# The feed-forward block by pairs of units, with the transposes ahead of a pair, a second ACT read of their bank, and later input loads

## The chip, the cores and the metric

The kernel runs on one core of a Trainium2 chip. It drives five engines: PE (matrix products, with a separate weight-load row PEld), DVE (vector), ACT (activations), POOL (GpSimd, which here issues weight loads and does a few additions) and SP (which issues most transfers). The metric is the time of one launch in device microseconds; lower is better. Three timed runs of the kernel before are at hand and one profiled execution.

## The reference

The input x is 2048 rows of 640 numbers, fp32. Everything after the layer norm works on the normalised rows:

```python
xn = _layernorm(x, axis=-1)
s = _A_ref(xn, A_wqkv, A_wo)          # attention, then @ wo
g = _silu(_B_ref(xn, B_w1, B_w2))     # silu(silu(xn @ w1) @ w2), 640 -> 1536 -> 640
return x + s * g
# in _A_ref: 32 heads of 20; each row attends to 8 rows, itself and every second row before it
qkv = x @ wqkv
logits = einsum("bhsd,bhswd->bhsw", q, kg) * 20 ** -0.5     # masked before row 0
o = einsum("bhsw,bhswd->bhsd", softmax(logits), vg)
return o @ wo
```

## The kernel before, in words

The 2048 rows are cut into four groups of 512 (two halves, even and odd rows). A group is worked as four tiles of 128 rows. Every product is computed to nearly fp32 precision from two halves, high and low: `TH` and `TL` hold the transposed activations (two copies of each, one for the present group and one for the next group or for the attention output), `WR` is a ring of seven slots, each with the high and low half of one weight unit, and a product is three matmuls: high by high, low by high, high by low.

A group goes through three phases on PE:

- `qkv_phase`: four quarters (8 heads each) of five chunks; a chunk is four tiles of three matmuls of 480 columns (L638 to L640). ACT reads the banks into `kv` and `q` (`evac_qkv`, L444 and L447), `halo` (L458 on) shifts rows between partitions by transfers, and `scores` and `values` (L481 to L521) compute the attention on DVE, with an exponential on ACT (L496) in between. In the quarters of a group the attention output of the group before is transposed chunk by chunk (`o_chunk`, placed by `O_AT`).
- `wo_phase`, from the second group on: the output projection of the group before, 20 tiles of six matmuls (L672 and L674). DVE multiplies the result by the gate `G` (L704), POOL adds x (L711), SP stores (L713).
- `ffn_phase`: 12 units f. An "up" (L791 to L793) is 15 matmuls of 512 columns into one of two `rot` banks; ACT reads the bank twice with silu, to `sh` (high half, L797) and `sf` (full, L798), and DVE subtracts to get `sl` (L799). A "down" multiplies `sh` (16 matmuls, "big") and then `sl` (8 matmuls, "small") into six `acc` banks, which hold the whole group's 512 by 640 result. Before the change the order on PE is up 0, up 1, down 0, up 2, down 1, and so on to up 11, down 10, down 11, so that up f is two units ahead of down f. At the end ACT takes the gate's silu out of the six banks (L828).

During `ffn_phase` the next group's five transposes of x are made, one before each of up 7 to up 11 (`split_t`: four PE transposes into a `rot` bank at L433, the high half by ACT at L437, the low half by DVE at L438 from the same bank). The last group has no next x; in the same way it transposes the attention output of its own group before up 8 to up 11 and before down 11 (`OL_AT`). The rows of the next group are loaded into `XIN` (`load_x`, L404) and normalised on DVE and ACT (`ln_stats`, `ln_rstd`, `ln_apply`).

No order is written out by hand for the engines other than PE. A planner, `Weave`, holds all operations with their reads, writes, a duration from a formula and a priority. PE's order is the program's; for DVE, ACT, POOL and SP it goes through time and takes at each step the operation that could start first, and among those the one of lowest priority number. The order that it finds is then fixed: on the chip each engine works through its list and waits where an operand is not ready. Priority 0 have the evacuations and `sl`, 1 the layer norm, 50 the splits of weights, 100 and up the attention.

Weight units are read from DRAM as fp32 (`raw_load`, L346, into `PR`, `RAW` and `G` early on, later `RAW` alone), split once by ACT (L372) and DVE or POOL (L378), stored as halves (L384), and read back as halves by POOL's queue when the unit comes again (L364). The tiles `XR` hold rows of x for the final addition (L710).

Of the kernel before, what the change touches and what calls it, by code (L numbers as in the profile page):

```python
# [8 lines left out]
F32 = mybir.dt.float32  # L9
# [5 lines left out]
P = 128  # L15
# [7 lines left out]
T = 4  # L23
# [10 lines left out]
HALVES = 1  # L34
BY_ACT = (1,)
QAT = 48
X_AT = 3, 6, 8
TILE_AT = 1, 1.5, 5, 6
LOW_AT = 3
# [134 lines left out]
def local_attention_silu_ffn(ctx: ExitStack, tc: tile.TileContext, x, wqkv, wo, w1, w2, out):  # L174
# [82 lines left out]
    def dma(fn, reads, writes, nbytes, prio, dur=0.45):  # L257
        add("SP", dur, fn, reads, writes, prio, nbytes=nbytes)
# [15 lines left out]

    units = []
    for g in range(NG):
        units += [("q", q, c) for q in range(NQ) for c in range(DC)]
        if g:  # L280
            units += [("wo", c) for c in range(DC)]
        for f in range(FC + 1):
            if f < FC:
                units.append(("w1", f))
            if f:
                units.append(("w2", f - 1))
    units += [("wo", c) for c in range(DC)]
    again = {u: sum(v == u for v in units) for u in units}
    halves = {}
# [25 lines left out]
    def raw_load(k):  # L315
# [7 lines left out]
        if k < DC:  # L323
            r, kr = PR.rearrange("p t w m -> p (t w m)")[:, k * n:(k + 1) * n], [PRK[k]]
        elif k < early:
            s = (k - DC) % 6
            r, kr = (RAW[s], [("raw", s)]) if s < 2 else (G[:, s - 2, :], [("g", s - 2, 0), ("g", s - 2, CA)])
            r = r[:, :n]
        else:
            s = k % 2  # L330
            r, kr = RAW[s][:, :n], [("raw", s)]
        raws[i] = r, kr
        if u[0] == "q":
            _, q, c = u
# [66 lines left out]


    def load_x(g, t, n=1, prio=None):
        dma(lambda: nc.sync.dma_start(XIN[:, t:t + n], rows(xg, g)[:, t:t + n]), [],  # L404
            [("xin", u) for u in range(t, t + n)], n * P * D * 4, clock[0] if prio is None else prio)

    def ln_stats(t, after=()):
# [19 lines left out]
    def split_t(src, skeys, c, i):  # L427

        ps, kp = rot()

        def turn():
            for t in range(T):
                nc.tensor.transpose(ps[:, tsl(t)], src[:, t, c * P:(c + 1) * P], ident)  # L433
# [3 lines left out]
        act(TOK, lambda: nc.scalar.activation(hi, ps, AF.Copy), [kp], kh, 0)  # L437
        dve(TOK, lambda: nc.vector.tensor_tensor(out=lo, in0=ps, in1=hi.bitcast(F32), op=OP.subtract),  # L438
            [kp] + kh, kl, 0)


    def evac_qkv(g, q, t, ps, kp):
# [181 lines left out]
    def qkv_phase(g, i, io):  # L624
        for q in range(NQ):
# [34 lines left out]
    OL_AT = {8: 0, 9: 1, 10: 2, 11: 3, 12: 4}  # L660
    XT_AT = 7

    def tm_banks():
        a = [bank() for t in range(T)]
# [99 lines left out]
        leave(t, B)  # L764

    def ffn_phase(g, i, ix, io):
        nxt = g + 1 if g + 1 < NG else None
        ps = prev = None
        for f in range(FC + 1):
            if nxt is not None and f == 0:  # L770
                load_x(nxt, 0, 2)
                load_x(nxt, 2, 2)
                for t in range(T):
                    ln_stats(t)
                ln_rstd(0, T)
                for t in range(T):
                    ln_apply(t)
            if nxt is not None and XT_AT <= f < XT_AT + DC:
                split_t(XIN, [("xin", t) for t in range(T)], f - XT_AT, ix)
            if nxt is None and f in OL_AT:  # L780
                o_chunk(g, OL_AT[f], io)
            cur = None
            if f < FC:
                wh, wl, kh, kl = w_next("w1", f)
                h, kp = rot()
                s = f % 2

                def first(wh=wh, wl=wl, h=h):
                    for c in range(DC):
                        cs = tsl(c)  # L790
                        nc.tensor.matmul(h, wh[:, cs], TH[i][:, c, :], start=c == 0, stop=False)  # L791
                        nc.tensor.matmul(h, wh[:, cs], TL[i][:, c, :], start=False, stop=False)  # L792
                        nc.tensor.matmul(h, wl[:, cs], TH[i][:, c, :], start=False, stop=c == DC - 1)  # L793
                pe(15 * mm(TOK), first, t_keys(i, range(DC)) + [kh, kl], [kp])
                w_done()
                sf, sh, sl = SF[s], SH[s], SL[s]
                act(TOK, lambda sh=sh, h=h: nc.scalar.activation(sh, h, AF.Silu), [kp], [("sh", s)], 0, "silu")  # L797
                act(TOK, lambda sf=sf, h=h: nc.scalar.activation(sf, h, AF.Silu), [kp], [("sf", s)], 0, "silu")  # L798
                dve(TOK, lambda sf=sf, sh=sh, sl=sl: nc.vector.tensor_tensor(  # L799
                    out=sl, in0=sf, in1=sh.bitcast(F32), op=OP.subtract), [("sf", s), ("sh", s)], [("sl", s)], 0, lock=True)  # L800
                cur = sh, sl, ("sh", s), ("sl", s)
            if f:
                sh, sl, ksh, ksl = prev
                if ps is None:
                    ps = tm_banks()
                a, b = ps
                wh, wl, kh, kl = w_next("w2", f - 1)
                for t in range(T):
                    def big(t=t, f=f, wh=wh, wl=wl, sh=sh):
                        tm_mm(ps, t, sh[:, tsl(t)], wh, f == 1, False)  # L810
                        tm_mm(ps, t, sh[:, tsl(t)], wl, False, False)

                    def small(t=t, f=f, wh=wh, sl=sl):
                        tm_mm(ps, t, sl[:, tsl(t)], wh, False, f == FC)
                    ko = [a[t][1], b[t // 2][1]]
                    pe(2 * TM, big, [ksh, kh, kl], ko)
                    if f == FC:
                        pe(TM, small, [ksl, kh], ko)
                    else:
                        late.append((TM, small, [ksl, kh], ko))  # L820
                for args in late:
                    pe(*args)
                late.clear()
                w_done()
            prev = cur
        for p, kp, ts, cs in tm_views(ps):
            n = (ts.stop - ts.start) * (cs.stop - cs.start)
            act(n, lambda p=p, ts=ts, cs=cs: nc.scalar.activation(G[:, ts, cs], p, AF.Silu), [kp], gkeys(ts, cs), 0, "silu")  # L828

    late = []  # L830
# [41 lines left out]
```

## Time and profile before

| what | value |
|---|---|
| timed runs | 641.08, 641.50, 641.52 us, median 641.5 |
| the profiled execution, its own time | 641.25 us |
| its span, first to last instruction | 639.5 us |
| granted PE clock | 1.000 |
| PE busy | 632.2 us |
| DVE busy | 540.1 us |
| ACT busy | 204.1 us |
| POOL busy | 122.3 us |
| transfers | 162.44 MB, mean 254 GB/s |

The span is what the profile's records cover; the execution's own time is 1.75 us longer. A row of a group view gives line, engine, operation, the tile written and the tile read, shapes, the count, the busy time, the mean duration of one, and the idle time of the engine just before with what ended it. In a timeline a row is a start, a duration and the same names. Successive instructions of one engine overlap a little in these records, on PE by design: the distance between starts, not the duration, is what a matmul costs there.

### The profile page before, as it was taken

To read this page: it belongs to the slowest core of one execution; us is meant where nothing else is said; L and a number is where in the kernel's file an instruction comes from. 1 tells how busy PE (TensorE), PEld (TensorE's weight loads), DVE (VectorE), ACT (ScalarE), POOL (GpSimd) and SP (SyncE) were. 2 spreads that over 40 slices of the span, in tenths; PEclk is the share of its full clock that TensorE was granted. 3 is DMA by queue.
4 is the path that set the end of the run, shared out by engine and by line. 5 is a ranking of instruction groups with operands and counts; after the bars stand their busy time and mean duration, and the time that the engine had idled before them with its cause. 6 is when DMAs were issued, how large, how long until landed. Compare 5 with 4: busy or idle time off the path is not lost.

```text
span 639.5 us, 9016 instructions
## 1 busy us (share of the span) xinstructions
PE 632.2 (99%) x3495; PEld 572.2 (89%) x3495; DVE 540.1 (84%) x539; ACT 204.1 (32%) x399; POOL 122.3 (19%) x168
## 2 busy tenths in 40 slices
PE   7999999999999999999999999999999999999997
PEld 6888889999889989999888999999988899899997
DVE  7699999999999899999859999999106999999714
ACT  5436453443524023232422112223313222233230
POOL 4500000001101241111222124311222213311100
PEclk9999999999999999999999999999999999999999
DMA  9999998787999998657699976965679996876522
GB/s 283 336 307 337 338 372 327 298 280 237 280 285 327 318 310 258 197 163 218 179 270 272 297 214 207 359 201 162 171 207 265 276 315 202 284 272 189 183 83 82
DMA packets 74154, 162.44 MB, mean 254 GB/s; under 512 B 5648, under 2 KB 47088, under 8 KB 74112
## 3 DMA queue, kind: packets, MB, share of 16 engines
q0 software_dynamic: 26672, 82.58, 44.7%
q1 hardware_dynamic: 46896, 78.88, 39.6%
q8 instruction: 27, 0.44, 0.3%
q10 hardware_dynamic: 544, 0.41, 0.2%
q14 instruction: 15, 0.12, 0.1%
HBM read 109.55 MB, written 34.16 MB: 225 GB/s over the span
## 4 chain that ended last, share of the span: by engine, by line
PE 97%; DVE 1%; DMA 1%; ACT 0%; issue 0%
PE acc L672 22%; PE acc L674 15%; PE acc L638 10%; PE acc L639 10%; PE acc L640 10%; PE rot L793 9%; PE rot L791 9%; PE rot L792 9%; PE rot L433 2%; PE acc L583 2%; DMA xin<-in_A_x_dram 1%; DVE st L548 1%; DVE xin L553 0%; PE rot L761 0%; PE rot L562 0%; DVE tl L570 0%
## 5 line engine op out<-in xcount | busy, mean ns | idle before, releaser
L638 PE MATMUL acc<-w,th 128*128 128x480 f32 x300 | 114.7, 382 | 0.0
L672 PE MATMUL acc<-w,sh 128*128 128x384 f32 x384 | 113.6, 335 | 0.0
L639 PE MATMUL acc<-w,tl 128*128 128x480 f32 x300 | 113.5, 378 | 0.0
L640 PE MATMUL acc<-w,th 128*128 128x480 f32 x300 | 113.4, 378 | 0.0
L674 PE MATMUL acc<-w,sh 128*128 128x256 f32 x384 | 107.1, 279 | 0.0
L481 DVE TENSOR_TENSOR pr<-q,kv 128x2560 f32<-128x2560 f32 x32 | 90.3, 2821 | 11.7 <-DMA kv<-kv 11.3
L791 PE MATMUL rot<-th,w 128*128 128x512 f32 x240 | 95.4, 398 | 0.0
L793 PE MATMUL rot<-th,w 128*128 128x512 f32 x240 | 94.0, 391 | 0.0
L792 PE MATMUL rot<-tl,w 128*128 128x512 f32 x240 | 93.8, 391 | 0.0
L513 DVE TENSOR_TENSOR pr<-e,kv 128x2560 f32<-128x2560 f32 x32 | 90.3, 2823 | 0.8
L484 DVE TENSOR_REDUCE l<-pr 128x128 f32<-128x2560 f32 x32 | 90.0, 2813 | 0.2
L364 POOL DMA_DIRECT2D w<-half_q x52 | 37.3, 717 | 233.4 <-PE rot L793 122.5
L518 DVE TENSOR_TENSOR pr<-pr 128x1280 f32<-128x1280 f32 x64 | 78.3, 1224 | 1.1
L797 ACT ACTIVATE sh<-rot 128x512 fp32r<-128x512 f32 x48 | 28.8, 599 | 151.5 <-PE rot L793 151.4
L674 PEld LDWEIGHTS acc<-w,sh 128*128 128x128 f32 x384 | 72.3, 188 | 1.6
L672 PEld LDWEIGHTS acc<-w,sh 128*128 128x128 f32 x384 | 72.1, 188 | 1.7
L364 POOL DMA_DIRECT2D w<-half_w x72 | 38.5, 535 | 182.0 <-PE acc L674 89.9
L640 PEld LDWEIGHTS acc<-w,th 128*128 128x128 f32 x300 | 56.3, 188 | 8.5
L638 PEld LDWEIGHTS acc<-w,th 128*128 128x128 f32 x300 | 56.3, 188 | 8.0
L639 PEld LDWEIGHTS acc<-w,tl 128*128 128x128 f32 x300 | 56.3, 188 | 8.0
L672 PE MATMUL acc<-w,sl 128*128 128x384 f32 x192 | 57.8, 333 | 0.0
L793 PEld LDWEIGHTS rot<-th,w 128*128 128x128 f32 x240 | 45.0, 188 | 9.9
(88 smaller groups left out, 975.0 us busy)
## 6 DMA issues: line engine op xcount, KB each, us to landing
w<-half_w POOLq DMA_DIRECT2D x72, 640.0 KB, 5.7
w<-half_q POOLq DMA_DIRECT2D x52, 480.0 KB, 5.4
half_w<-w SPq DMA_DIRECT2D x24, 640.0 KB
half_q<-w SPq DMA_DIRECT2D x20, 480.0 KB
w<-half_wo POOLq DMA_DIRECT2D x15, 640.0 KB, 5.5
kv<-kv SPq DMA_DIRECT2D x16, 560.0 KB
kv<-kv SPq DMA_DIRECT2D x16, 420.0 KB
gate<-in_B_w_dram SPq DMA_DIRECT2D x16, 320.0 KB
```

The source lines that it names most:

```text
L481: dve(2560, lambda t=t: nc.vector.tensor_tensor(out=PR, in0=win(qq[:, t:t + 2, :], W, 0), in1=win(kv[:, 0, t:t + 2, :], W, CQ), op=OP.mult ...
L484: dve(2560, lambda t=t: nc.vector.tensor_reduce(out=l[:, t:t + 2].rearrange("p t w h -> p (t w h)"), in_=PR.rearrange("p t w (h d) -> p (t ...
L513: dve(2560, lambda t=t, v=v: nc.vector.tensor_tensor(out=PR.rearrange("p t w (h d) -> p t (w h) d", d=DH), in0=e[:, t:t + 2].rearrange("p ...
L518: dve(2 * n * CQ, lambda n=n: nc.vector.tensor_tensor(out=PR[:, :, 0:n, :], in0=PR[:, :, 0:n, :], in1=PR[:, :, n:2 * n, :], op=OP.add), [] ...
L638: nc.tensor.matmul(o, hi, wh, start=c == 0, stop=False)
L639: nc.tensor.matmul(o, lo, wh, start=False, stop=False)
L640: nc.tensor.matmul(o, hi, wl, start=False, stop=c == DC - 1)
L672: nc.tensor.matmul(a[t][0][:, :CA], st, w[:, :CA], start=first, stop=last)
L674: nc.tensor.matmul(b[t // 2][0][:, h * CB:(h + 1) * CB], st, w[:, CA:], start=first and h == 0, stop=last, skip_group_check=True)
L791: nc.tensor.matmul(h, wh[:, cs], TH[i][:, c, :], start=c == 0, stop=False)
L792: nc.tensor.matmul(h, wh[:, cs], TL[i][:, c, :], start=False, stop=False)
L793: nc.tensor.matmul(h, wl[:, cs], TH[i][:, c, :], start=False, stop=c == DC - 1)
```

## The change

`ffn_phase` now walks a list, `plan(g)`. For the first three groups the list is up 0, up 1, down 0, down 1, then for each later pair: one transposed chunk ("turn"), up, up, down, down. The five turns stand before the pairs 2/3 to 10/11. The last group goes by pairs up to unit 5, then returns to the old alternation with its turns where they were. The weight units are requested in the new order, since `units` is built from the same list.

In the turns of `ffn_phase` for the next x, ACT reads the bank twice: to `TH` as before, and as a full copy into a new tile `XT`; DVE's subtraction for `TL` reads `XT` instead of the bank, and is marked as one that shares its port with POOL (`lock`). The tiles `XT` take the room of `RAW`, and the early loads of weights go to `XR` in place of `RAW`.

`load_x` for the next group now reads a key "gone", whose writer is the last PE operation of the second quarter (`LOAD_AT = 1`) of the present group: the transfer waits for it.

```diff
-    RAW = tiles("raw", 2, [P, D])
+    XT = tiles("xt", 2, [P, TOK])
...
+    def plan(g):
+        if g < NG - 1:
+            return [s for f in range(0, FC, 2) for s in ([("turn", f // 2 - 1)] if f else []) +
+                    [("up", f), ("up", f + 1), ("down", f), ("down", f + 1)]]
+        n = FC - DC - 1
+        p = [s for f in range(0, n, 2) for s in (("up", f), ("up", f + 1), ("down", f), ("down", f + 1))] + [("up", n)]
+        for f in range(n + 1, FC):
+            p += [("turn", f - n - 2)] if f > n + 1 else []
+            p += [("up", f), ("down", f - 1)]
+        return p + [("turn", DC - 1), ("down", FC - 1)]
...
-            r, kr = (RAW[s], [("raw", s)]) if s < 2 else (G[:, s - 2, :], [("g", s - 2, 0), ("g", s - 2, CA)])
+            r, kr = (XR[s], [("xr", s)]) if s < 2 else (G[:, s - 2, :], [("g", s - 2, 0), ("g", s - 2, CA)])
...
-        dma(lambda: nc.sync.dma_start(XIN[:, t:t + n], rows(xg, g)[:, t:t + n]), [],
+        dma(lambda: nc.sync.dma_start(XIN[:, t:t + n], rows(xg, g)[:, t:t + n]), ["gone"],
...
-        dve(TOK, lambda: nc.vector.tensor_tensor(out=lo, in0=ps, in1=hi.bitcast(F32), op=OP.subtract),
-            [kp] + kh, kl, 0)
+        if via is None:
+            x, kx = ps, kp
+        else:
+            x, kx = XT[via], ("xt", via)
+            act(TOK, lambda: nc.scalar.activation(x, ps, AF.Copy), [kp], [kx], 0)
+        dve(TOK, lambda: nc.vector.tensor_tensor(out=lo, in0=x, in1=hi.bitcast(F32), op=OP.subtract),
+            [kx] + kh, kl, 0, lock=via is not None)
...
+            if q == LOAD_AT:
+                wv.writer["gone"] = [o for o in wv.ops[-40:] if o.eng == "PE"][-1]
...
+            order = [(t, k) for k in (0, 1) for t in range(T)]
+            for t, low in sorted(order) if f == FC - 1 else order:
+                give(t, low)
+            w_done()
+
+        for k, n in plan(g):
+            {"up": up, "down": down, "turn": turn}[k](n)
```

The bodies of `up` and `down` are those of the loop before: the same matmuls in the same order within a unit.

More of the change, by code (lines that the diff above doesn't have):

```diff
@@ L36 @@
 QAT = 48
+LOAD_AT = 1
 X_AT = 3, 6, 8
@@ L766, in ffn_phase @@
     def ffn_phase(g, i, ix, io):
[L767 to L825, printed above, removed]
@@ new lines, in ffn_phase, with turn, up, first @@
+        last = g == NG - 1
+        if not last:
+            load_x(g + 1, 0, 2)
+            load_x(g + 1, 2, 2)
+            for t in range(T):
+                ln_stats(t)
+            ln_rstd(0, T)
+            for t in range(T):
+                ln_apply(t)
+        banks = []
+        def turn(c):
+            if last:
+                o_chunk(g, c, io)
+            else:
+                split_t(XIN, [("xin", t) for t in range(T)], c, ix, c % 2)
+        def up(f):
+            wh, wl, kh, kl = w_next("w1", f)
+            h, kp = rot()
+            s = f % 2
+            def first():
+                for c in range(DC):
+                    cs = tsl(c)
+                    nc.tensor.matmul(h, wh[:, cs], TH[i][:, c, :], start=c == 0, stop=False)
+                    nc.tensor.matmul(h, wh[:, cs], TL[i][:, c, :], start=False, stop=False)
+                    nc.tensor.matmul(h, wl[:, cs], TH[i][:, c, :], start=False, stop=c == DC - 1)
+            pe(15 * mm(TOK), first, t_keys(i, range(DC)) + [kh, kl], [kp])
+            w_done()
+            sf, sh, sl = SF[s], SH[s], SL[s]
+            act(TOK, lambda: nc.scalar.activation(sh, h, AF.Silu), [kp], [("sh", s)], 0, "silu")
+            act(TOK, lambda: nc.scalar.activation(sf, h, AF.Silu), [kp], [("sf", s)], 0, "silu")
+            dve(TOK, lambda: nc.vector.tensor_tensor(out=sl, in0=sf, in1=sh.bitcast(F32), op=OP.subtract),
+                [("sf", s), ("sh", s)], [("sl", s)], 0, lock=True)
@@ L826, in ffn_phase @@
+        for k, n in plan(g):
+            {"up": up, "down": down, "turn": turn}[k](n)
+        ps = banks
         for p, kp, ts, cs in tm_views(ps):
```

28 lines of the change are left out of this document (18 added, 10 removed).

## The prediction

> **What bounds the kernel now.** I read the page's busy shares first, then PE's waits, then stretches of the span, then the PE timeline of one unit.
>
> ```profile
> span 639.5 us, 9016 instructions
> PE 632.2 (99%) x3495; PEld 572.2 (89%) x3495; DVE 540.1 (84%) x539; ACT 204.1 (32%) x399; POOL 122.3 (19%) x168
> ```
> ```profile
> PE rot L562 <- DVE xin L553: 1.8, 3, 0.9
> PE rot L536 <- POOL ident masks.py:199: 1.4, 1, 1.4
> PE acc L583 <- DVE tl L570: 0.3, 1, 0.3
> ```
> ```profile
> 63.10:148.10 85.00, 85.00 (x490) 77.52 (x490) 81.99 (x77) 38.94 (x65) 3.02 (x4) 1.00 0.91 325
> 219.80:304.50 84.70, 84.70 (x490) 77.29 (x489) 80.13 (x80) 23.88 (x39) 20.12 (x28) 1.00 0.75 231
> 376.50:461.20 84.70, 84.70 (x489) 77.27 (x489) 71.32 (x64) 25.16 (x40) 22.78 (x28) 1.00 0.68 215
> ```
>
> The second block is everything that PE's matmuls waited for: 3.5 us, all on lines of the opening. The stretches (columns: length, then busy time of PE, PEld, DVE, ACT, POOL, the clock, transfers) are the feed-forward phases of groups 0, 1 and 2, and PE is busy in every moment of them. Busy could still hide a slow pace, so here is one unit:
>
> ```profile
> 260.95 0.34 PE L672 MATMUL acc<-w,sh 128*128 128x384 f32 x1
> ...
> 263.26 0.33 PE L672 MATMUL acc<-w,sl 128*128 128x384 f32 x1
> ...
> 264.41 0.60 PE L433 MATMUL rot<-ident,xin 128*128 128x128 f32 x4
> 264.76 0.48 PE L791 MATMUL rot<-th,w 128*128 128x512 f32 x1
> ...
> 268.05 0.39 PE L793 MATMUL rot<-th,w 128*128 128x512 f32 x1
> 268.28 0.34 PE L672 MATMUL acc<-w,sh 128*128 128x384 f32 x1
> ```
>
> A down starts at 260.95 and ends where the turn starts, 264.41: 3.46 us, of which the 16 matmuls on `sh` take 2.31. Turn and up together take 3.87, up to 268.28; the last of the 15 matmuls follows its forerunners at the even pace of 0.23 us, and four transposes add about 0.44, so an up is 3.43. Nothing here waits for a bank, a weight or `sl`.
>
> So the change can win only outside PE's stream: 639.5 − 632.2 = 7.3 us of PE idle, all at the head and the tail. It can lose wherever a lead that is now long becomes short.
>
> **The change part by part**, against the profiled run's 641.25 us.
>
> *The matmuls and transposes themselves: 0.* Each unit, and each of the 15 turns, keeps its instructions; they only change places. Two ups in a row or two downs in a row meet without a gap in the rows above as well as their mixture does. Bounds −0.2 to +0.2 us; I take 0.
>
> *ACT's second read of the bank: 0.* Fifteen copies by the row of their sister, the high half:
>
> ```profile
> L437 ACT ACTIVATE th<-rot 128x512 fp32r<-128x512 f32 x35 | 20.9, 597 | 74.7 <-PE rot L433 74.5
> L438 DVE TENSOR_TENSOR tl<-rot,th 128x512 fp32r<-128x512 f32 x35 | 23.9, 684 | 35.3 <-ACT th L437 35.1
> L799 DVE TENSOR_TENSOR sl<-sf,sh 128x512 fp32r<-128x512 f32 x48 | 36.3, 756 | 16.1 <-ACT sf L798 16.0
> ```
>
> 15 × 0.597 = 9.0 us on ACT, which is busy 24 of 84.7 us in this phase. The up that follows the turn covers it: ACT needs 1.2 us after the turn, PE works 3.43 on the other bank before it wants this one again. On DVE the subtraction from SBUF is like `sl`'s: 15 × (0.756 − 0.684) = 1.1 us more in the whole run. Without that cover a turn would cost at most 1.2 us, 18 in all. The bank was never what PE waited for, so no wait goes away either. I take 0.
>
> *The order by pairs: the leads shrink.* Before, between the end of up f and down f stand another down and another up, 6.9 us; `sl` is wanted 2.31 later, after 9.2. After, only one unit stands between, for even f the second up and for odd f the first down: 3.43 us for `sh`, 5.74 for `sl`. Measured from the recorded end of the last matmul (268.44 above, 0.16 after the next unit's start), and with the weight load 0.19 ahead of its matmul, it is about 3.1 and 5.4.
>
> ```profile
> L674 PEld LDWEIGHTS acc<-w,sh 128*128 128x128 f32 x384 | 72.3, 188 | 1.6
> ```
>
> What do ACT and DVE need? The slowest of the 48 units, f = 8 of group 2, and the next, f = 4 of group 0:
>
> ```profile
> 432.07 0.39 PE L793 MATMUL rot<-th,w 128*128 128x512 f32 x1
> ```
> ```profile
> 432.62 0.42 ACT L496 ACTIVATE e<-l 128x256 f32<-128x256 f32 x1 [1.67 <-DVE l L494]
> 433.06 1.28 ACT L797 ACT_TABLE_LOAD   x1
> 434.36 0.60 ACT L797 ACTIVATE sh<-rot 128x512 fp32r<-128x512 f32 x1
> 434.85 0.59 ACT L798 ACTIVATE sf<-rot 128x512 f32<-128x512 f32 x1
> ```
> ```profile
> 434.61 2.82 DVE L513 TENSOR_TENSOR pr<-e,kv 128x2560 f32<-128x2560 f32 x1
> 437.35 0.69 DVE L799 TENSOR_TENSOR sl<-sf,sh 128x512 fp32r<-128x512 f32 x1
> ```
> ```profile
> 90.24 0.39 PE L793 MATMUL rot<-th,w 128*128 128x512 f32 x1
> ```
> ```profile
> 95.33 0.68 DVE L799 TENSOR_TENSOR sl<-sf,sh 128x512 fp32r<-128x512 f32 x1
> ```
>
> PE's up ends at 432.46; an exponential is in ACT's way, then the table for silu must be loaded, `sh` is there 2.50 us after the end, `sl` 5.58, because DVE had just begun a product of 2.82. In group 0 it is 96.01 − 90.63 = 5.38. So even before, two units in 48 needed the whole of what the new order leaves, with nothing lost since 9 us were to be had.
>
> The Trainium skill (ScalarE: Activation LUTs, "What ACT_TABLE_LOAD costs") puts a switch of tables at 1283 ns of loading plus about 1380 ns of draining. The row agrees with the load (1.28) and not with the drain, since the silu starts 0.02 us after it. By the page `sh` would come 2.66 + 0.64 = 3.3 us after the end of an up that follows an exponential.
>
> Will the new order meet such cases? The built order of the changed kernel lists DVE's work between successive `sl`. By the mean durations
>
> ```profile
> L481 DVE TENSOR_TENSOR pr<-q,kv 128x2560 f32<-128x2560 f32 x32 | 90.3, 2821 | 11.7 <-DMA kv<-kv 11.3
> L484 DVE TENSOR_REDUCE l<-pr 128x128 f32<-128x2560 f32 x32 | 90.0, 2813 | 0.2
> L518 DVE TENSOR_TENSOR pr<-pr 128x1280 f32<-128x1280 f32 x32 | 49.1, 1534 | 0.3
> L518 DVE TENSOR_TENSOR pr<-pr 128x640 f32<-128x640 f32 x32 | 29.3, 914 | 0.8
> ```
>
> (the products on `e` as those on `q`, the smaller kinds from 0.35 to 0.76) a pair holds 9 to 14 us of DVE work beside its two `sl`, against 14.2 of PE. Tightest is group 1: from `sl` 3, where DVE is idle, to `sl` 8 stand 40.8 us of other work and five `sl` of 0.69, 44.3; PE goes from the end of up 3 to that of up 8 in 39.2. So `sl` 8 would start 1.15 + 44.3 − 39.2 = 6.2 us after its up, and end 6.9 after: 1.5 too late. Started operations overlap, though: 434.61 + 2.82 is 437.43, and the next starts at 437.35. With 0.04 to 0.08 less for each, the start is 4.7 and the end 5.4, just in time. Bounds 0 to 1.5 us; I take 0.25, by the second reckoning, since applied to the old order it puts `sl` 4 of group 0 at 4.75 after its up, and the records have 95.33 − 90.63 = 4.70. The next tightest ends are 5.0 (group 3, f = 4) and 4.8 (group 1, f = 4), by the same count; a stall there starts only from half a us of further delay. For `sh`, the exponential that is nearest to an up (group 0, f = 4) comes 0.8 us ahead of its end, and 0.4 is what it needs: bounds 0 to 1, I take 0.05. The end of group 1's phase gets an exponential and a table load ahead of ACT's six gate reads, which free the banks for the next phase:
>
> ```profile
> L828 ACT ACTIVATE gate<-acc 128x384 f32<-128x384 f32 (+1 forms) x24 | 11.4, 526 | 12.5 <-PE acc L672 12.5
> ```
>
> The scores are reduced about 3.0 after the end of up 11; with 0.42 and 1.28 for exponential and load and 0.5 a read, the first bank is free at 5.2 and PE wants it at 6.7, after two downs. The closest, the fourth read, leaves 1.4 us: bounds 0 to 1.5, I take 0.05.
>
> *The loads held back: 0 to 1.5, I take 0.1, and 0.1 for the first group.* Two transfers of 640 KB for each of three groups move past the queue. SP stood still for them before, after PE's last turn:
>
> ```profile
> SPq L404 <- PE rot L433: 31.6, 2, 29.5
> ```
>
> Now they wait for the end of the second quarter, and queued behind them on SP are the shifts of that quarter, which wait for the same moment. Layer norm on DVE moves from the start of a group into its third quarter. What it can delay is the gate multiplication ahead of down 0:
>
> ```profile
> 377.46 2.83 DVE L481 TENSOR_TENSOR pr<-q,kv 128x2560 f32<-128x2560 f32 x1
> 380.20 3.14 DVE L704 TENSOR_TENSOR gate<-acc,gate 128x384 f32<-128x384 f32 x6
> ```
> ```profile
> 383.14 0.34 PE L672 MATMUL acc<-w,sh 128*128 128x384 f32 x1
> ```
>
> Six multiplications end at 383.3, and down 0, which needs the first bank at 383.1 and the last 1.3 later, just does not wait. For the new order I added DVE's list in group 2 from where the shifted rows of the first quarter land,
>
> ```profile
> 330.98 2.83 DVE L481 TENSOR_TENSOR pr<-q,kv 128x2560 f32<-128x2560 f32 x1 [6.40 <-DMA kv<-kv]
> ```
>
> with layer norm in, `z`, `e`, one reduction and one product out, and the gates again start at 380.1. The cover is 1.3 us. In group 0 the same sum puts `sl` 0 about 4.2 after its up, 1.2 inside its lead. POOL's additions of x for the first output, and their loads, which used to be issued at the start, come later too; the ring lets a weight be late by six units, some 20 us, so that costs 0.
>
> The head up to 12 us is the same list on every engine: 0.
>
> Sum: 641.25 + 0.25 + 0.05 + 0.05 + 0.1 + 0.1 = 641.8, with 0.2 for unnamed short waits of the same kinds 642.0. The median of the runs shown lies 0.25 above the profiled run, well inside the roughly 0.2% (1.3 us) that a measurement can tell; I leave the forecast at **642.1**.
>
> **The rivals.**
> 1. *The leads break (slower).* If DVE runs 1 us later than the second reckoning, `sl` is late wherever less than that is left: in groups 0, 1 and 3, each at its worst unit. A stall gives DVE time, so a group pays about once. 3 × 1 to 1.5 us: 645. It decides from 0.5 us of delay. For: two units needed 5.4 and 5.6 before. Against: 44 of 48 were done by 4.9.
> 2. *The held-back rows land late (slower).* DVE's list stands still for them in order. Landing 4 us after DVE reaches them costs 4 − 1.3 in group 2, and as much in group 0: 5.4, so 647; 2 us late 643.3. For: the transfer engines are at 0.98 and 1.06 in the stretches of quarters and output product. Against: by the sums above 5 to 12 us lie between issue and use, where a weight unit of the same size takes 5.7.
>
> ```profile
> 148.10:219.80 71.70, 71.70 (x381) 64.44 (x380) 67.91 (x72) 24.97 (x56) 8.91 (x14) 1.00 0.98 288
> 304.50:376.50 72.00, 72.00 (x383) 64.71 (x382) 60.67 (x50) 17.66 (x45) 15.85 (x25) 1.00 1.06 259
> ```
> ```profile
> w<-half_w POOLq DMA_DIRECT2D x72, 640.0 KB, 5.7
> ```
>
> 3. *Nothing at all (same).* No lead breaks: 641.5.
> 4. *The head gains (faster).* Less early traffic lets first weights land sooner: at most 3.5 us of PE waits there, 639 if a large part went; but they name DVE and POOL, not transfers, and come before the lists differ.
> 5. *A table load holds ACT for twice its row (slower).* Then `sh` comes 2 × 1.28 + 0.64 = 3.2 us after an up against 3.1, and about ten silus follow an exponential: 10 × 0.1 on the forecast, 643. Against it speaks the 0.02 between load and silu. With the drain of the Trainium skill's page (ScalarE: Activation LUTs) each would cost 0.2, and the time be 644.
>
> **How the numbers follow.** Forecast with short stalls 0.50, rival 3 0.10, rival 1 0.22, rival 2 0.12, rival 4 0.04, rival 5 0.02. Rivals 1, 2 and 5 make slower, 0.36; the forecast and 3 are within 0.2%, 0.60; faster 0.04. The range leaves out rival 4 and the far part of rivals 1 and 2: 641.2 to 644.2. The forecast's own range is 641.2 to 642.8.
>
> **What would show it.** PE's stretches of the three phases stay within half a us of 85.0, 84.7 and 84.7. PE's waits gain rows on L672 released by `sl` or `sh`, short, most in group 1. ACT's `rot` reads by copy number 30 in `ffn_phase`, and no PE wait names them. DVE is still idle at times in each phase. Wrong would be a PE wait on a weight transfer, a wait of 1 us or more at a down, or a span below 638.5.

## The result, and the profile after

The changed kernel takes 644.3 us (median of six runs, 642.27 to 645.5), the kernel before 641.22 us beside it (641.08 to 641.52): a ratio of 1.0043, with an interval of 1.0032 to 1.0054. It is slower, by about 3 us. About 0.35 of that lies outside the span: in all six runs the execution's own time is 2.1 us above the span of its records, where it was 1.75 before, and no record shows what fills it. The profiled run is the longest of the six, 645.5 us, so the stalls below are near the upper end of what the runs show.

The page of the changed kernel, its span and its engines:

```profile
span 643.4 us, 9045 instructions
PE 633.2 (98%) x3495; PEld 572.6 (89%) x3495; DVE 535.5 (83%) x539; ACT 216.0 (34%) x418; POOL 125.9 (20%) x168
```

The span grew by 3.9 us, and PE does the same 3495 matmuls in nearly the same busy time. So there are new waits. PE's waits, the whole list (us in total, times, longest):

```profile
PE acc L687 <- DVE sl L815: 3.3, 3, 1.5
PE rot L551 <- POOL ident masks.py:199: 1.4, 1, 1.4
PE rot L577 <- DVE xin L568: 0.9, 3, 0.4
PE acc L689 <- ACT q L462: 0.4, 1, 0.4
PE acc L598 <- DVE tl L585: 0.3, 1, 0.3
```

The first row is the lead that broke (L687 is the down, L815 the subtraction that makes `sl`), the fourth is a bank that ACT read late; the others are the opening, as before. The feed-forward phases of groups 0, 1 and 2, from the first up to the next phase (length, then busy time of PE, PEld, DVE, ACT, POOL, the clock, transfers):

```profile
62.96:150.76 87.80, 85.10 (x489) 77.34 (x488) 84.91 (x83) 43.67 (x75) 3.02 (x4) 1.00 0.93 318
223.12:307.65 84.53, 84.53 (x490) 77.38 (x489) 81.33 (x75) 28.59 (x46) 23.09 (x29) 1.00 0.73 230
379.83:464.38 84.55, 84.55 (x490) 77.37 (x489) 75.23 (x68) 27.59 (x45) 21.07 (x28) 1.00 0.69 216
```

The same stretches of the kernel before:

```profile
62.94:147.81 84.87, 84.87 (x489) 77.42 (x488) 81.86 (x77) 38.90 (x64) 3.02 (x4) 1.00 0.91 325
219.65:304.48 84.83, 84.83 (x491) 77.42 (x489) 80.26 (x80) 23.88 (x39) 20.12 (x28) 1.00 0.75 231
376.31:461.16 84.85, 84.85 (x490) 77.42 (x489) 71.51 (x64) 25.16 (x40) 22.78 (x28) 1.00 0.68 215
```

Groups 1 and 2 are 0.30 us *shorter* than before; group 0 is 2.9 longer. The longest stall, down 2 of group 0, on PE and then on DVE:

```profile
87.59 0.28 PE L689 MATMUL acc<-w,sh 128*128 128x256 f32 x1
89.40 0.44 PE L687 MATMUL acc<-w,sl 128*128 128x384 f32 x1 [1.53 <-DVE sl L815]
```
```profile
85.92 2.82 DVE L528 TENSOR_TENSOR pr<-e,kv 128x2560 f32<-128x2560 f32 x1
88.66 0.68 DVE L815 TENSOR_TENSOR sl<-sf,sh 128x512 fp32r<-128x512 f32 x1
```

DVE started a product of 2.82 us just ahead of `sl`. The lead can be measured now. Where PE stalled at a down, the table sets the end of `sl`, counted from the recorded end of the last matmul of its up, beside the stall (the distance between starts of the matmuls above, less the 0.12 of an even pace):

| kernel, unit | `sl` ends after its up, us | PE's stall, us | difference |
|---|---|---|---|
| changed, group 0, f = 0 | 6.81 | 1.33 | 5.48 |
| changed, group 0, f = 2 | 7.18 | 1.69 | 5.49 |
| changed, group 3, f = 4 | 6.28 | 0.79 | 5.49 |
| changed, group 1, f = 8 | 5.07 | none | |

The lead is 5.49 us, and whatever `sl` needs beyond it is lost in full. The bookkeeping closes: 1.33 + 1.69 + 0.79 at downs, 0.59 at the output product of group 0 (at 205 us, where PE waits for ACT's read of a bank, and ACT has just waited 5.35 us for a raw weight of `wo`) and 0.35 in a quarter of group 2 (349 us) make 4.75; three phases save 0.3 each; 4.75 − 0.9 is 3.85, and the span grew by 3.9. (Three groups go by pairs throughout; where the 0.3 comes from stands in the last section.)

Why was DVE late in group 0? ACT's waits between 36 and 75 us, of the changed kernel:

```profile
ACT w L381 <- DMA xr<-in_B_w_dram: 3.9, 2, 1.9
ACT w L381 <- DMA gate<-in_B_w_dram: 2.9, 1, 2.9
```

and of the kernel before, the rows that name a landing of raw weights:

```profile
ACT w L372 <- DMA gate<-in_A_wqkv_dram: 0.6, 1, 0.6
ACT w L372 <- DMA gate<-in_B_w_dram: 0.2, 1, 0.2
```

For raw weights of the feed-forward (`in_B_w`) ACT waits 6.8 us where it waited 0.2; for those of the attention it is 0.5 against the 0.6 above. ACT works its list in order, so everything behind such a split is late, as this stretch of ACT in the changed kernel shows:

```profile
64.25 0.74 ACT L381 ACTIVATE w<-xr 128x640 fp32r<-128x640 f32 x1 [1.95 <-DMA xr<-in_B_w_dram]
64.90 0.42 ACT L459 ACTIVATE kv<-acc 128x320 f32<-128x320 f32 x1
...
67.72 1.28 ACT L813 ACT_TABLE_LOAD   x1
69.01 0.60 ACT L813 ACTIVATE sh<-rot 128x512 fp32r<-128x512 f32 x1
```

PE has ended the quarter by 62.96, where its first up begins; the first read of the quarter's banks starts at 64.90, because the split ahead of it waited for a transfer. The reading of this, tested below: the transfer is late because the held-back rows of x now go out after the second quarter, ahead of the shifts and the weights, as SP's own queue in the changed kernel shows:

```profile
37.85 2.56 SPq L413 DMA_DIRECT2D xin<-in_A_x_dram  x2
40.51 3.62 SPq L473 DMA_DIRECT2D kv<-kv  x4
44.23 5.75 SPq L355 DMA_DIRECT2D gate<-in_B_w_dram  x3
```

Before the change the same rows left at 12 and 20 us. The transfer engines now stand partly idle just ahead of the held rows. The stretch from 23.4 to 36.4 us, changed kernel, then before (the last two numbers are the transfers' share and GB/s):

```profile
23.40:36.40 13.00, 13.00 (x62) 11.29 (x61) 8.02 (x6) 4.49 (x12) 9.34 (x6) 1.00 0.79 220
```
```profile
23.40:36.40 13.00, 13.00 (x62) 11.28 (x61) 10.85 (x16) 4.79 (x13) 9.76 (x6) 1.00 1.08 288
```

From 36.4 to 63.1 us the share is 1.04 to 1.09 in both kernels, and there the two loads of 640 KB, 1.3 MB, are now added. The 68 GB/s of difference are not the held rows alone: two kernels below whose rows leave early have 243 and 232 GB/s in this stretch. What the rows do to the transfers behind them shows in the completion times of the traces. In group 0, for all raw weight loads of the feed-forward that SP issued from 43 to 49.5 us:

| kernels | rows of x land, at the latest, us | a raw weight load takes, us |
|---|---|---|
| before, and the eight variants below whose rows leave early in group 0 | 26.2 to 28.6 | 4.2 to 7.3 |
| changed | 50.5 | 10.3 to 11.6 |
| the four variants below with the rows held to the second quarter | 47.7 to 52.0 | 8.3 to 12.7 |

Held and not held do not overlap. In the changed kernel the next two loads are issued late as well (50.6 and 56.1 us, against 48.0 and 48.5 in the first experiment). On DVE, between 36 and 75 us, the lateness shows as waits of 1.5 us for the rows of x and 1.1 for splits that ACT had made late. DVE, too, did layer norm in the stretch from 23.4 to 36.4 us before (16 operations against 6).

### The profile page after: what moved, and what is told of

Read it like the earlier page. It is cut to its first block, busy times and chain, and to the rows that moved or that the text cites. A ratio compares the mean times of both kernels' runs of the same rounds, so it can differ in the third digit from the quotient of the medians.

```text
span 643.4 us, 9045 instructions
## 1 busy us (share of the span) xinstructions
PE 633.2 (98%) x3495; PEld 572.6 (89%) x3495; DVE 535.5 (83%) x539; ACT 216.0 (34%) x418; POOL 125.9 (20%) x168
## 4 chain that ended last, share of the span: by engine, by line
PE 79%; DMA 9%; DVE 6%; SPq 2%; ACT 2%; issue 1%; DVEq 0%; ACTq 0%
PE acc L687 20%; PE acc L689 14%; PE rot L807 7%; PE rot L809 7%; PE rot L808 7%; PE acc L653 7%; PE acc L654 7%; PE acc L655 7%; DMA kv<-kv 4%; DMA xin<-in_A_x_dram 2%; PE rot L443 2%; PE acc L598 2%; SPq L473 2%; DVE pr L496 1%; DVE l L499 1%; DMA xr<-in_B_w_dram 1%
## 5 line engine op out<-in xcount | busy, mean ns | idle before, releaser
L687 PE MATMUL acc<-w,sh 128*128 128x384 f32 x384 | 113.3, 334 | 0.0
L533 DVE TENSOR_TENSOR pr<-pr 128x1280 f32<-128x1280 f32 x64 | 73.9, 1155 | 1.2
L687 PEld LDWEIGHTS acc<-w,sh 128*128 128x128 f32 x384 | 72.1, 188 | 1.1
L687 PE MATMUL acc<-w,sl 128*128 128x384 f32 x192 | 58.2, 335 | 3.3 <-DVE sl L815 3.3
L447 ACT ACTIVATE th<-rot 128x512 fp32r<-128x512 f32 x35 | 20.9, 597 | 110.8 <-PE rot L443 110.8
```

The source lines that it names most:

```text
L687: nc.tensor.matmul(a[t][0][:, :CA], st, w[:, :CA], start=first, stop=last)
```

## The experiments

The theory to test: with pairs the leads are short (5.49 us), but what breaks them is the held-back loads. Its rivals: the order alone breaks them; or ACT's second read of the bank, more work in ACT's list, is what delays. Every edit makes the planner write all the lists anew, so differences between two kernels are not strictly additive; the median of the runs and one profile are given for each, the ratios are against the kernel before.

**Loads not held back, all else of the change kept.**

```diff
-        dma(lambda: nc.sync.dma_start(XIN[:, t:t + n], rows(xg, g)[:, t:t + n]), ["gone"],
+        dma(lambda: nc.sync.dma_start(XIN[:, t:t + n], rows(xg, g)[:, t:t + n]), [],
```

> The changed kernel with the input loads of the next group free again (no wait for the second quarter's end). Theory A (the order by pairs halves the leads, and the first group's DVE and ACT are late for reasons of their own, weights that land late): the stalls at down 0 and down 2 of group 0 stay, 643.5 to 645. Theory B (layer norm in the third quarter and the loads beside the shifts make DVE late in group 0): both stalls go or fall under 0.3 us, 641.3 to 642.3, with about 0.8 left in group 3 and 0.6 in the output product.

641.72 us (640.53 to 642.45, 11 runs), ratio 1.0002 [0.9994, 1.0011]. The profile (span 638.9) has one PE wait beyond the opening's:

```profile
PE acc L687 <- DVE sl L815: 0.2, 1, 0.2
```

It is down 4 of group 3, whose `sl` ends at 5.86 and costs 0.37: 5.49 again. ACT waits for no raw weight between 36 and 75 us. So without the hold nearly all of the loss goes, 2.6 of 3 us by the medians.

**The old alternation in all groups, with held-back loads and ACT's second read.**

```diff
     def plan(g):
+        if True:
+            p, n = [("up", 0)], FC - DC if g < NG - 1 else FC - DC + 1
+            for f in range(1, FC):
+                p += [("turn", f - n)] if f >= n else []
+                p += [("up", f), ("down", f - 1)]
+            return p + ([("turn", DC - 1)] if g == NG - 1 else []) + [("down", FC - 1)]
```

> The changed kernel with the old alternation of ups and downs in all groups; held-back loads and the second ACT read stay. Both A and B: no PE wait on sl or sh, since 9 us are there again, 641.0 to 641.8. If the held-back loads cost PE something directly (a late weight or a late gate), it shows here as more than 641.8.

643.53 us (642.85 to 643.7, 5 runs), ratio 1.0035 [1.0022, 1.0048]: far more than expected, and without pairs. PE waits for no `sl`, though `sl` ends as late as 6.75 and 7.04 after its up in group 0: with the long lead of the old order that costs nothing. The cost comes by another way. PE's new wait in this kernel:

```profile
PE acc L659 <- ACT q L468: 0.8, 1, 0.8
```

It is in the third group's quarters. There ACT, in order:

```profile
346.01 0.42 ACT L517 ACTIVATE e<-l 128x256 f32<-128x256 f32 x1 [11.93 <-DVE l L515]
...
346.81 0.43 ACT L465 ACTIVATE kv<-acc 128x320 f32<-128x320 f32 x1
```

and DVE, which feeds that exponential:

```profile
342.90 0.88 DVE L426 BATCH_NORM_STATS2 st<-xin 128x6 f32<-128x320 f32 x2
...
344.93 0.58 DVE L513 TENSOR_REDUCE m<-l 128x32 f32<-128x256 f32 x1
345.55 0.43 DVE L515 TENSOR_TENSOR l<-l,m 128x256 f32<-128x256 f32 x1
```

Held-back rows bring layer norm into the quarters; two of its tiles, 2.0 us, stand on DVE ahead of the two small operations that the exponential needs; and behind the exponential on ACT stand the reads of the quarter's banks. PE loses 0.99 there, between the starts of two matmuls. The changed kernel has the same at 347.93 us: an exponential that waited 11.19 us for DVE, ahead of the bank reads, and PE's 0.35 at 349 us. So the held-back loads cost in the old order too.

**The old alternation in group 0 alone.** (The same insertion, with `if g == 0:`.)

> The old alternation in group 0 alone, pairs in groups 1 and 2 and in the first half of group 3. If the loss sits in group 0, as the profile has it (3.0 of 4.6 us), 641.8 to 643.0; if pairs cost in every group, 643 or more.

643.28 us (641.89 to 645.55, 11 runs), ratio 1.0028 [1.0017, 1.0038]. Group 0 has no stall left; gaps of 0.78 (down 4 of group 3), 0.43 (output product, 202 us) and 0.32 (a quarter of group 2) remain. Group 0's broken leads are about 1 us of the median's loss; with a loss that sits in group 0 it should have come to 643.0 at most. The gaps that remain are in the later groups.

**DVE reads the bank, as before the change; all else kept.**

```diff
-                split_t(XIN, [("xin", t) for t in range(T)], c, ix, c % 2)
+                split_t(XIN, [("xin", t) for t in range(T)], c, ix)
```

> The changed kernel with the transposes' bank read by ACT and DVE as before (one ACT read, DVE from the bank). Theories A and B: no difference beyond the planner's reshuffling, 643.5 to 645. Rival C, that fifteen copies of 0.6 us in ACT's list and the subtraction from SBUF delay sh and sl: 642 to 643.

643.73 us (641.52 to 649.13, 12 runs), ratio 1.0052 [1.003, 1.0074]. The profiled run is the longest, and shows a wait that the changed kernel doesn't have:

```profile
PE rot L807 <- DVE tl L453: 2.5, 1, 2.5
```

On DVE, at that place:

```profile
86.15 0.68 DVE L453 TENSOR_TENSOR tl<-rot,th 128x512 fp32r<-128x512 f32 x1
```

The second up of a pair wants the bank that the turn filled, 3.4 us after the turn; DVE frees it at 86.83, PE's first matmul of that up starts at 86.89 and could have started at 84.28. So in this order the bank can be what PE waits for. What ACT's second read is worth on the whole this kernel doesn't show: its median is no worse than the changed kernel's, and 1.0 us of its profiled run is a late clock (last section).

**The order alone: loads free, DVE reads the bank.** (Both edits together.)

> Pairs alone: loads free, the transposes' bank read by ACT and DVE as before. Theory A (the shorter leads cost by themselves): 642.5 or more. Theory B (the held-back loads make almost the whole loss): 641.2 to 642.2, as pairs with the second ACT read and free loads had 641.7. If the second ACT read guards the bank, as the 2.6 us wait of an up for DVE's subtraction in the held-back variant suggests, this is up to 0.7 above that 641.7.

644.63 us (643.35 to 646.15, 6 runs), ratio 1.0044 [1.003, 1.0058]: as slow as the whole change, and in the range of the expectation's theory A, that the order costs by itself. Its profiled run is its fastest, and its waits beyond the opening are

```profile
PE acc L653 <- ACT gate L845: 0.7, 1, 0.7
PE acc L687 <- DVE sl L815: 0.6, 1, 0.6
PE rot L807 <- DVE tl L453: 0.5, 2, 0.3
```

The last row is the bank again. The first is a place that the prediction had priced: the reads of the gate out of the `acc` banks, at the end of group 1's phase. ACT there:

```profile
302.50 0.49 ACT L845 ACTIVATE gate<-acc 128x384 f32<-128x384 f32 x1 [1.83 <-PE acc L687]
303.01 1.28 ACT L426 ACT_TABLE_LOAD   x1
304.31 0.30 ACT L426 ACTIVATE sd<-mv,epst 128x4 f32<-128x4 f32 x1
304.62 1.28 ACT L845 ACT_TABLE_LOAD   x1
305.92 2.24 ACT L845 ACTIVATE gate<-acc 128x384 f32<-128x384 f32 x5
```

A square root of layer norm stands between the first gate read and the other five, with a table load on either side: 2.9 us. Two of the three parts together, pairs and ACT's read, are even (the first experiment); pairs alone are not. But little of it is the short lead: by the distances between starts, PE loses 0.82 at the bank, 0.87 at the gate reads and 0.77 at down 4 of group 3. What the other five runs, up to 2.8 us longer, waited for isn't known from one profile.

**ACT's second read alone: old alternation, loads free.** (The edits of the first and the second experiment.)

> The second ACT read (with the early weights in XR) alone: old alternation, loads free. Theory (each part matters only through leads that are too short): 641.0 to 641.7, no PE wait behind the opening, since the old order leaves 9 us for sl. If the ACT read or the shared XR costs by itself, 642 or more.

641.78 us (641.54 to 643.55, 11 runs), ratio 1.0008 [0.9999, 1.0018]; no PE wait beyond the opening's, and a span of 639.4. Alone, the read and the move of the weight loads to `XR` give nothing, and cost at most little: the median span of its runs is that of the kernel before, 639.4 us, and the 0.6 between the medians lies outside the span (2.34 us there, 1.78 before).

**Only the first held-back load held; only the later two held.**

```diff
-        dma(lambda: nc.sync.dma_start(XIN[:, t:t + n], rows(xg, g)[:, t:t + n]), ["gone"],
+        dma(lambda: nc.sync.dma_start(XIN[:, t:t + n], rows(xg, g)[:, t:t + n]), ["gone"] if g == 1 else [],
```

(`g == 1` is the load that is issued in group 0; the second kernel has `g > 1` in its place.)

> The changed kernel, with only the load that is issued in group 0 held back; the two later ones free. If group 0 makes the loss (3.0 of 4.6 us of the new PE gaps), 643 to 644.5; if the later groups do (exponentials late behind the layer norm, ACT's bank reads queued behind them), 641.5 to 642.3.

> The mirror: the load in group 0 free, the loads in groups 1 and 2 held back. Group 0 to blame: 641.5 to 642.3. Later groups to blame: 642.5 to 644. The sum of the two excesses over 641.7 should come near the changed kernel's 2.6.

The first: 643.99 us (642.9 to 645.89, 6 runs), ratio 1.0039 [1.0024, 1.0053], with stalls of 0.34 and 1.81 at downs 0 and 2 of group 0, and ACT waiting 7.4 us for raw weights of the feed-forward; DVE waits for no rows of x there. Its profile also has 1.31 at the gate reads after group 1 and 0.65 at down 4 of group 3, where no load is held, so only half of its gaps are group 0's. The second: 643.49 us (642.13 to 644.82, 6 runs), ratio 1.0025 [1.0012, 1.0038]; group 0 is clean, and 0.7 to 0.8 each are lost at a quarter of group 2, at a down of group 1 and at down 4 of group 3. Its profiled run has a further 1.1 us in the opening, from a late clock (last section). Above the kernel with free loads the medians are 2.3 and 1.8, together more than the 2.6 of both, where the expectation had them add up: each of the two kernels loses, but not all that they lose comes from the load that is held.

**The transfer early, layer norm held back.**

```diff
-                ln_stats(t)
+                ln_stats(t, ("gone",))
```

(with free loads, as in the first experiment)

> The transfers free, but the layer norm's statistics wait for the second quarter's end. Theory B1 (the cost is the layer norm's place in DVE's list, among scores and exponentials): 643 to 644.5, as the changed kernel. Theory B2 (the cost is the transfer's place: 1.3 MB beside shifts and weights that ACT and DVE then wait for): 641.3 to 642.2.

642.71 us (642.02 to 645.19, 11 runs), ratio 1.0025 [1.0015, 1.0036], between the two ranges of the expectation. Group 0 has no stall, and ACT waits 1.8 us for raw weights, which take 5.0 to 6.0 us each: in group 0 it is the transfer's place that costs, not layer norm's. What is left is 0.86 at down 4 of group 3, and 1.42 at the gate reads after group 1, as in the next kernel.

**The loads held back to the first quarter only.**

```diff
-LOAD_AT = 1
+LOAD_AT = 0
```

> The changed kernel with the loads held to the end of the first quarter in place of the second. Theory B2 (in group 0 the transfer leaves the queues underused before 36 us and crowds the weights after): the transfer now falls into the gap, the stalls at down 0 and down 2 of group 0 go (ACT's waits for landing weights between 36 and 75 us fall from 6.8 to under 3), 641.8 to 643.3. Theory B1 (the layer norm's place in DVE's list): group 0 stays as it was, 643.5 to 645.

642.91 us (642.45 to 644.49, 11 runs), ratio 1.0023 [1.0014, 1.0033]. The stretch from 23.4 to 36.4 us again:

```profile
23.40:36.40 13.00, 13.00 (x62) 11.30 (x61) 10.23 (x21) 4.19 (x11) 9.35 (x6) 1.00 0.89 261
```

The transfers fill it better than in the changed kernel (220 GB/s), the raw weights take 5.4 to 6.4 us, ACT waits for none, and group 0 loses 0.14. So the mechanism in group 0 stands. Left are 0.77 at down 4 of group 3 and PE's wait for the gate reads of group 1, behind which ACT shows:

```profile
304.09 1.28 ACT L511 ACT_TABLE_LOAD   x1
305.38 0.42 ACT L511 ACTIVATE e<-l 128x256 f32<-128x256 f32 x1
305.82 1.28 ACT L845 ACT_TABLE_LOAD   x1
```

This time an exponential with its two table loads, 3.0 us, stands between the gate reads, and PE, at 306.02, loses 1.42. This stall comes with the loads free (the order alone; the transfer early), with the first held to the second quarter, and here; the changed kernel hasn't got it. So it goes with the lists that the planner writes rather than with the loads, and the medians of these variants contain it.

**Pairs in groups 0 to 2, the old alternation in group 3, loads free, ACT's second read kept.** (The insertion of the second experiment with `if g == NG - 1:`.)

> Loads free, second ACT read, pairs in groups 0 to 2, the old alternation in group 3 throughout. The stall of 0.4 to 0.9 at down 4 of group 3, which every variant with pairs there shows, goes: 641.0 to 641.6, at the kernel before within 0.1%. If it is slower than pairs with free loads (641.7), the planner's new lists cost elsewhere what the order gains.

640.88 us (640.45 to 643.67, 11 runs) against 641.18 before, ratio 0.9997 [0.9986, 1.0007]. The last stall, down 4 of group 3, is gone; PE's waits are those of the opening alone, and the phases of groups 0 and 2 are

```profile
62.85:147.43 84.58, 84.58 (x490) 77.35 (x488) 82.99 (x81) 41.41 (x68) 3.02 (x4) 1.00 0.93 326
...
375.68:460.22 84.54, 84.54 (x491) 77.36 (x490) 71.35 (x63) 27.60 (x45) 20.41 (x28) 1.00 0.67 216
```

0.29 and 0.31 shorter than before, and the span is 638.5 against 639.5. By the median of the runs the span is 0.6 shorter, but 2.10 us lie outside it where 1.78 did, and 0.3 is left in the time. This is the best version found, and all that the order by pairs has been seen to give; the interval does not exclude no change.

**Pairs for units 0 to 3 of group 3 as well.**

```diff
-        n = FC - DC - 1
-        p = [s for f in range(0, n, 2) for s in (("up", f), ("up", f + 1), ("down", f), ("down", f + 1))] + [("up", n)]
-        for f in range(n + 1, FC):
-            p += [("turn", f - n - 2)] if f > n + 1 else []
+        n = FC - DC + 1
+        p = [s for f in (0, 2) for s in (("up", f), ("up", f + 1), ("down", f), ("down", f + 1))] + [("up", 4)]
+        for f in range(5, FC):
+            p += [("turn", f - n)] if f >= n else []
```

(with free loads)

> Loads free, second ACT read, pairs in groups 0 to 2, and in group 3 pairs only for units 0 to 3, the alternation from unit 4 on. Theory (pairs save PE some 0.05 us at each change between up and down that they avoid, 0.3 per phase, and cost only where sl comes more than 5.5 us after its up, which in group 3 was unit 4): no PE wait on sl, group 3's phase 0.1 shorter than with the alternation throughout (84.9 for 85.0), 640.6 to 641.2, below the kernel before. If the lead is short wherever pairs stand in group 3, a new wait shows at down 0 to 3 and the time is 641.2 or more.

642.11 us (641.16 to 642.98, 12 runs), ratio 1.0008 [1.0, 1.0017]: a miss. In the profile `sl` 4 of group 3 ends 5.82 after its up and costs 0.33; the rest of that run's difference in span is the clock in the opening (last section). Of the 0.8 by which the median lies above the kernel before, about 0.35 is outside the span, as in the changed kernel. No gain from pairs in that group was found.

## Where the prediction was right and where wrong, point by point

Forecast were short stalls, 642.1 us, with 641.2 to 642.8 for that case and 641.2 to 644.2 with the near part of the rivals. It became 644.3: at the upper end of the wide range, 0.1 above it, and slower by more than a measurement can confuse. That the time came out so near the range is owed to the room left for rivals, not to the mechanism forecast: the term that made the loss was put at 0.1 and 0.1.

- *PE's stream bounds the kernel, and the change can lose wherever a long lead becomes short:* right. The growth of the span is the sum of PE gaps with a releaser, less what the pairs save. What lies outside the span, 0.35 us, the prediction took as fixed. That the change could win only outside PE's stream was wrong: the pairs save 0.9 inside it, as the next point says.
- *The matmuls and transposes themselves, 0 (−0.2 to +0.2):* the sign is now known. Pairs save 0.30 per phase, 0.9 in three groups, beyond the bound given. I had looked at whether units meet without a gap, not at the pace within them. The rows shown held no two ups in a row; the trace before has such a place, up 1 after up 0, and up 1 takes 3.40 us there against the 3.43 that I used.
- *ACT's second read, 0, "the bank was never what PE waited for":* right for the order before. In the new order it was the wrong question: with DVE's read the second up of a pair can wait for the bank, up to 2.6 us; so the second read can be worth something only together with the pairs. That the cover was "the up that follows the turn" held in the changed kernel.
- *The leads, 3.1 and 5.4:* 5.49 for `sl`, as reckoned. The list of tight units was half right: group 1's f = 8, forecast 5.4, came at 5.07; group 3's f = 4, forecast 5.0, at 6.28, 5.86 even with free loads. There a product of 2.83 us began just ahead of `sl`, as the DVE row of the changed kernel shows:

```profile
570.10 2.83 DVE L496 TENSOR_TENSOR pr<-q,kv 128x2560 f32<-128x2560 f32 x1
572.85 1.28 DVE L815 TENSOR_TENSOR sl<-sf,sh 128x512 fp32r<-128x512 f32 x2
```

  In a list of operations of 2.8 us an error of a few tenths decides on which side of such an operation a small one comes; the term of 0.25 had the right size for this (0.37 with free loads), but by luck: it was reckoned for another unit, which did not stall.
- *An exponential and a table load ahead of the gate reads, 0.05, "the closest leaves 1.4 us":* no wait in the profile of the changed kernel, but 0.9 to 1.4, between starts of matmuls, in four of its variants. It is the bound of 1.5 that was to be believed. On the rival of the table load: after it the silu at 69.01 starts 0.01 us behind the load, so the drain that the Trainium skill adds (ScalarE: Activation LUTs, "What ACT_TABLE_LOAD costs") doesn't show here either.
- *The loads held back, "I take 0.1, and 0.1 for the first group":* this is the step that failed. It cost 2.6 us by the medians, 4.7 by the profiled runs, above the 1.5 given as the upper bound. I followed the held transfers to layer norm and the gates on DVE, and asked what SP had queued behind them; I did not ask what their 1.3 MB take from the raw weights of the next units (10.3 to 11.6 us from issue to landing, 4.6 to 6.0 without the hold), which ACT waits for in order, with the bank reads and silus behind. For the ring I had reckoned six units of slack; that holds for weights that come back as halves, not for the splits in group 0. And in the later groups I followed layer norm to the gates, not to the exponential whose delay holds up ACT's reads of the banks.
- *Rival 2, the rows land late:* near in price (644.3 lies inside its 643.3 to 647), but only in part in mechanism. Down 0 lost by `sl`, not by the gates. DVE did wait for rows of x in group 0, 1.5 us in all and no more than 1.1 at once, so a part of this rival is in the loss; but with only the first load held, DVE waited for no rows and down 2 lost 1.81. *Rival 1, the leads break:* they did, in groups 0 and 3. In group 0 they were set off by the loads; in group 3 down 4 waits 0.3 to 0.9 in every kernel with pairs there, the loads free or not. The chances treated the two rivals as separate; in group 0 the late transfers were the cause of the broken leads.
- "A wait of 1 us or more at a down" was named as what would refute the forecast; there were two.

What stays open: why the runs of one variant differ by 0.9 to 7.6 us where those of the kernel before differ by 0.4 beside the changed kernel and by 1.9 to 2.4 beside the variants (the clock in the opening, last section, makes a part of it; landing times in group 0 may make another, but only one run of each has a profile); what fills the time outside the span; and how much of the later groups' loss is layer norm's place and how much the transfers'.

## What to carry to other kernels

When a transfer is held back, count what it will share the transfer engines with at its new place, and follow each of those to the engine that takes it in order: what is queued there behind a late landing pays, even if it has nothing to do with the transfer. A shorter lead doesn't show its price alone; it turns every small delay elsewhere into lost time, so price both together. Where an edit lets a planner rewrite the lists, test it with each of its partners, not alone.

## What the runs showed of the hardware

Two things were not expected. First, an up is shorter after an up than after a down: 3.40 against 3.45 us between first matmuls (medians over the units of the phases, from the records), though no wait stands between them; in a phase six ups follow an up where one did, and the five more give 5 × 0.047 = 0.24. A down is shorter after a down than after an up, too, 3.441 against 3.453, and five more follow one: 0.06. Together that is the 0.30 that the phases save. Whether the change of shape from 256 columns to 512 or the change of banks costs it was not tried.

Second, the granted PE clock can fall to one half for a moment in the opening. Three stretches of 1 us from 9 to 12 us, the first and the last, in the profiled run with pairs up to unit 3 of group 3 (the last three numbers are clock, transfers' share and GB/s), and two matmuls there:

```profile
9.00:10.00 1.00, 1.00 (x3) 0.87 (x4) 0.96 (x5) 1.00 (x3) 0.00 (x0) 0.50 1.12 319
...
11.00:12.00 1.00, 1.00 (x4) 0.87 (x3) 0.90 (x2) 0.00 (x0) 0.00 (x0) 0.50 1.09 345
```
```profile
9.33 0.60 PE L598 MATMUL acc<-w,th 128*128 128x480 f32 x1
9.73 0.60 PE L598 MATMUL acc<-w,tl 128*128 128x480 f32 x1
```

The matmuls come at 0.40 us where 0.22 is the pace of the same ones at full clock. The stretch of 8 to 9 us has a clock of 0.97 and that of 12 to 13 one of 0.82, so the half clock lasts 0.06 + 3 + 0.36 = 3.4 us, and takes 1.7 us of PE's work away; the opening of that run is 1.7 us longer than that of the kernel with pairs in three groups. The Trainium skill (TensorE: Matmul & The Clock Gate, "What's actually happening") has the clock set to half or full by windows of about 3.4 us that run on their own; this length agrees. Such executions can be told by a mean clock of 0.996 or 0.997 in place of 0.999 or 1.000: of the 17 runs of the kernel before beside it, the three with the lower figure took 642.24 to 642.88, the others 640.95 to 641.95. They occur among the runs of nearly every kernel here and widen the ranges above. The mean doesn't show every slow opening: in the profiled runs with DVE reading the bank (loads held) and with the later two loads held, it is 0.999 and 1.000, yet the matmuls come at 0.40 us from about 9 to 10.4, the records of the full clock begin only at 10.8 and 10.7 (at 4.3 to 7.3 in all others), and the first up comes 1.0 to 1.1 us later than with the loads free.
